# Moving the value sums of a pair of heads to the opening run of the next iteration, with their evacuation and one lower half

## Chip, core, metric

The kernel runs on one core of a Trainium2 chip. The metric is the device time of one execution in microseconds; the time before is 981.24 us, the median of three runs (979.43 to 981.75).

## The reference

Two independent computations, joined along the last axis. Part A is an attention with 32 heads of width 18 over 2048 rows in four segments of 512. Each segment has a causal softmax inside it, plus a lookup in a memory that is summed over the segments before. Part B is a Fourier mixing: two dense matrix products, one over 576 columns and one over 2048 rows. The core of it:

```python
# A: per segment s and head h (L = 512, Dh = 18)
logits = einsum("bhqd,bhkd->bhqk", qs, ks) * Dh**-0.5 + mask   # mask = -1e9 where key > query
a_dot  = einsum("bhqk,bhkd->bhqd", softmax(logits), vs)
a_mem  = einsum("bhld,bhde->bhle", phi(qs), M) / (einsum("bhld,bhd->bhl", phi(qs), z)[..., None] + 1e-6)
o      = sigmoid(beta) * a_mem + (1 - sigmoid(beta)) * a_dot
M, z   = M + phi(ks)^T vs, z + sum(phi(ks))
outA   = concat(o) @ wo
# B
a, b = x @ dft_hid_re.T, x @ dft_hid_im.T
outB = dft_seq_re @ a - dft_seq_im @ b
out  = concatenate([outA, outB], axis=-1)
```

## The kernel before

The first 217 us project queries, keys and values, sum the memory and look it up. From there to about 918 us two things run interleaved: the dense products of part B (`hidden`, then `sequence`, first for the real and then for the imaginary matrix) and the softmax attention of part A. An output stage ends the kernel.

The order is written out by hand. `attention()` is a generator: iteration p works on several pairs of heads at once, each in another stage, and yields eight times. At each yield the main loop makes a tick (which runs what `later(n, ...)` has queued n ticks before), takes what `PLAN` names for that slot, and then puts dense products on TensorE until their share of the work has caught up with the slot's weight in `SLOTS`. So what stands in the text between two yields is issued together, and dense products fill the space between. Of the eight places only two issue TensorE work of the attention in every iteration: the code before the second yield (here called slot 1, the opening run, which begins with `s_fill`) and the code before the fifth (slot 4).

A pair is one even and one odd head. For both, `scores` makes the scores in the PSUM banks `s0`, `s1`, `t0`, `t1`, and `smallest` (line 982, VectorE) takes the row minima of the negated scores. Two groups of heads share the steps:

- Even heads form transposed exponentials. `t_fill` makes the scores and ScalarE their exponentials in `pf` and `phi`; `t_mask` (GpSimd) masks the diagonal blocks; `t_hi` and `t_lo` write the higher halves `phi` and the lower halves `plo` in 16 bits. `t_lo(n, 0)` is VectorE's subtraction over 512 columns, the first lower half; `t_lo(n, 1)` is VectorE's over 384 columns and reads a PSUM bank; `t_lo(n, 2)` runs on GpSimd.
- Odd heads form exponentials with queries on the partitions (`f_fill`, `f_exp`), split them into `hl` (`f_split_hi`, `f_split_lo`) and turn them by a transposing DMA into `ptt` (`f_turn`, on the sync queue).

`pv(n)` (lines 1102, 1103) makes the value sums of one head, 10 products of 55 and 10 of 37 columns; both heads of a pair share the PSUM bank `pv`, of which there is one (`bufs=1`). `pv_out` (lines 1115 to 1124, five VectorE instructions) divides the sums and adds them to the output tile `og`; after the second pair of a group it queues `turn_out`, which transposes `og` (line 1137, VectorE), copies a tail (GpSimd) and sends both out by DMA. A new `pv` may start only when the last instruction of the previous `pv_out` is done.

VectorE has other work in the same stream. The halves of the second Fourier matrix (line 124, `h_split` through `PLAN`, iterations 21 to 29) and the lower halves of `hidden` (line 94) are two. The subtractions of the dense result from the first product (line 654) and the differences for the output stage (lines 744, 715) are the others.

Of the kernel before, what the change touches and what calls it, by code (L numbers as in the profile page):

```python
# [40 lines left out]
def infini_attention_and_fnet(ctx: ExitStack, tc: tile.TileContext, xT, wqk, w8, wv, wo, beta, xtT, cT, hT, out):  # L41
# [46 lines left out]
    def later(n, fn, *a):  # L88
        due.setdefault(clock[0] + n, []).append((fn, a))
# [374 lines left out]
    def stacks(p_, i):  # L464
        qs_bufs.append(p_.tile([P, 4, L], BF16, name=f"qs{i}"))
        ks_bufs.append(p_.tile([P, 4, L], BF16, name=f"ks{i}"))
        pool.memset(ks_bufs[i].bitcast(F32)[96:], BF16_ONES)
# [19 lines left out]

    def stack_load(G):
        if G < NG:
            s, g8 = divmod(G, 8)  # L490
            rows = slice(g8 * 72, g8 * 72 + 72)
            for n, (buf, src) in enumerate(((ks_bufs, kd), (qs_bufs, qd))):
                later(1 + n, dma, buf[G % 4][:NPAIR], src[s][rows].rearrange("(h d) c t -> (d c) h t", d=DH))

    def value_load(G):
        if G < NG:
            s, g8 = divmod(G, 8)
            VS[G] = sa.tile([P, 4, 220], BF16, name="vst", bufs=2)
            dma(VS[G], vd[s][:, :, g8])
# [65 lines left out]
    def bank(name, shape, dtype, tag):  # L565
        turns[tag] ^= 1
        return ps.tile(shape, dtype, name=name, tag=f"{tag}{turns[tag]}", bufs=1)
# [397 lines left out]
    def scores(n, kind, tag="s"):  # L965
        G, h = divmod(n, 4)
        q, k = qs_bufs[G % 4][:NPAIR, h], ks_bufs[G % 4][:NPAIR, h]
        if kind == 2 and SHARED:
            o = SHARED.pop()
        else:  # L970
            o = bank("s", [P, L], F32, tag)
            if kind == 2:
                SHARED.append(o[:, 256:])
        for i, c in ROWS[kind]:
            w = (i + 1) * P
            pe.matmul(o[:, c:c + w], q[:, i * P:w], k[:, :w], start=True, stop=True)  # L976
        return o
# [7 lines left out]
    def s_fill(n, kind, o=None):  # L985
        G, h = divmod(n, 4)
        smallest(scores(n, kind) if o is None else o, kind, -1.0, NEGM[G % 2][:, 2 * h:2 * h + 4])
# [3 lines left out]
    def f_fill(n, kind, o=None):  # L991
        if o is None:
            o = scores(n, kind, "s" if kind else "t")
        if kind == 1:
            F_[n] = [sa.tile([P, 4], F32, name="nb", bufs=2), sa.tile([P, 1280], F32, name="pf", bufs=3), {}]
        smallest(o, kind, -SCALE, F_[n][0])
        F_[n][2][kind] = o
# [27 lines left out]
    def maxima(G):  # L1025
        m, b = NEGM[G % 2].rearrange("p (h n) -> p h n", h=2), MB[G % 2][:, :24].rearrange("p (h c n) -> p c h n", h=2, c=3)
        r = sa.tile([P, 2, 4], F32, name="negx", bufs=2)
        pool.tensor_copy(b[:, 0], m)
        pool.tensor_tensor(r, m, b[:, 0], OP.subtract)
        pool.tensor_copy(b[:, 1], r)  # L1030
        pool.tensor_tensor(b[:, 2], r, b[:, 1], OP.subtract)

    def maxima_transpose(G, o):
        t = o[:, 384:512]
        pe.matmul(t, MB[G % 2], ident16, start=True, stop=True)
        yield
        w = sa.tile([24, P], BF16, name="mt", bufs=2)
        act.activation(w, t[:24], AF.Copy)
        for h in range(2):
            later(1, dma, qs_bufs[G % 4][NPAIR:NPAIR + 3, 2 * h].rearrange("c (n t) -> c n t", n=4), w[12 * h:12 * h + 12])  # L1040
# [64 lines left out]
    def pv_out(n2):  # L1105
        G, hh = divmod(n2, 2)
        s, g8 = divmod(G, 8)
        o = PV.pop(n2)
        og = OG[G % 2]
        h0 = 4 * g8 + 2 * hh  # L1110
        w = o[:, 440:].rearrange("p (h i c) -> p h i c", h=2, c=1)
        b = o[:, :144].rearrange("p (h i d) -> p h i d", h=2, i=4)
        o = o[:, :440].rearrange("p (h i c) -> p h i c", h=2, i=4)
        a = sa.tile([P, 8, DH], F32, name="pa", bufs=2)
        dve.reciprocal(w, o[:, :, :, 54:])
        dve.tensor_tensor(w, w, g1[:, h0:h0 + 2, None, None].to_broadcast([P, 2, 4, 1]), OP.mult)
        dve.tensor_reduce(a, o[:, :, :, :54].rearrange("p h i (c d) -> p (h i) d c", c=3), axis=AX, op=OP.add)
        to = og[:, :, 36 * hh:36 * hh + 36].rearrange("p i (h d) -> p h i d", d=DH)
        a = a.rearrange("p (h i) d -> p h i d", h=2)
        if s == 0:  # L1120
            dve.tensor_tensor(to, a, w.to_broadcast([P, 2, 4, DH]), OP.mult)
        else:
            dve.tensor_tensor(b, a, w.to_broadcast([P, 2, 4, DH]), OP.mult)
            dve.tensor_tensor(to, to, b, OP.add)
        if hh == 1:
            later(6, turn_out, G)
# [33 lines left out]
    F_LAG, T_LAG, V_LAG = 2, 3, 4  # L1160
    NP = 2 * NG
    SLOTS = (1060.0, 890.0, 1060.0, 660.0, 890.0, 1060.0, 650.0, 1210.0)

    def attention():
        for p in range(NP + V_LAG):
            def even(lag, fn, *a):
                if 0 <= p - lag < NP:
                    fn(2 * (p - lag), *a)

            def odd(lag, fn, *a):  # L1170
                if 0 <= p - lag < NP:
                    fn(2 * (p - lag) + 1, *a)

            if p < 2:
                OG.append(sa.tile([P, 4, 72], F32, name=f"og{p}"))
            if p == 0:
                stack_load(1)
                later(20, value_load, 0)
            if p % 2 == 0:
                later(39, value_load, p // 2 + 1)  # L1180
                later(30, memory_load, p // 2)
            even(T_LAG + 1, t_lo, 0)
            odd(F_LAG + 1, f_split_hi)
            yield SLOTS[0]
            G = p // 2 - 1 if p % 2 == 0 and 0 < p <= NP else None
            even(0, s_fill, 0)
            even(T_LAG, t_fill, 0)
            even(T_LAG, t_fill, 1, G)
            even(0, s_fill, 1)
            if G is not None and p < T_LAG:  # L1190
                list(maxima_transpose(G, bank("trm", [P, L], F32, "t")))
            odd(F_LAG + 1, f_split_lo, pool, 512, 1280)
            yield SLOTS[1]
            even(T_LAG, t_lo, 1)
            odd(F_LAG + 1, f_split_lo, dve, 0, 512)
            yield SLOTS[2]
            if p < 2:
                stacks(sq, p + 2)
            even(T_LAG, t_mask)
            yield SLOTS[3]  # L1200
            SHARED.clear()
            both = {}
            odd(F_LAG, f_fill, 1)
            even(0, lambda n: both.update(s=scores(n, 2)))
            odd(F_LAG, lambda n: both.update(f=scores(n, 2)))
            even(0, lambda n: s_fill(n, 2, both["s"]))
            odd(F_LAG, lambda n: f_fill(n, 2, both["f"]))
            even(V_LAG, pv)
            odd(V_LAG, pv)
            even(T_LAG, t_fill, 2)  # L1210
            odd(F_LAG, f_fill, 0)
            yield SLOTS[4]
            if p % 2 and p < NP:
                maxima(p // 2)
            odd(F_LAG + 1, f_turn)
            if p % 2:
                if p == 1:
                    later(6, stack_load, 2)
                else:
                    stack_load((p + 3) // 2)  # L1220
                if 2 < p < 18:
                    later(2, copy_parts, 2, 7 + p // 2)
            elif 4 <= p < 36:
                later(2, copy_parts, 3, (p - 4) // 2)
            even(T_LAG, t_hi)
            yield SLOTS[5]
            odd(F_LAG, f_exp, 1, 2, 0)
            even(T_LAG, t_lo, 2)
            yield SLOTS[6]
            if V_LAG <= p < NP + V_LAG - 1:  # L1230
                pv_out(p - V_LAG)
            yield SLOTS[7]

    d = dense()
# [6 lines left out]
    for n, w in enumerate(attention()):  # L1241
        tick()
        ta += w
        for fn, a in PLAN.pop(n, ()):
            fn(*a)
        while td / total_d < ta / total_a:
            t = next(d, BREAK)
            if t is BREAK:
                break
            td += t  # L1250
# [56 lines left out]
```

## Time and profile before

| what | value |
| --- | --- |
| median of three runs | 981.24 us |
| the profiled execution, own time | 982.62 us |
| its span, first to last instruction | 980.9 us |
| TensorE busy | 973.3 us (99%) |
| VectorE busy | 749.8 us (76%) |
| ScalarE busy | 680.8 us (69%) |
| GpSimd busy | 663.1 us (68%) |
| granted TensorE clock | 1.0 |
| DMA queue 1, share of 16 engines | 84.8% |

Busy is the union of the recorded instructions. TensorE's ends are modelled, so 99% says that it is rarely without an instruction, not that it runs at its peak. The 1.72 us between the execution's time and its span lie before the first and after the last instruction.

### The profile page before, as it was taken

To read this page: it belongs to the slowest core of one execution; us is meant where nothing else is said; L and a number is where in the kernel's file an instruction comes from. 1 tells how busy PE (TensorE), PEld (TensorE's weight loads), DVE (VectorE), ACT (ScalarE), POOL (GpSimd) and SP (SyncE) were. 2 spreads that over 40 slices of the span, in tenths; PEclk is the share of its full clock that TensorE was granted. 3 is DMA by queue.
4 is the path that set the end of the run, shared out by engine and by line. 5 is a ranking of instruction groups with operands and counts; after the bars stand their busy time and mean duration, and the time that the engine had idled before them with its cause. 6 is when DMAs were issued, how large, how long until landed. Compare 5 with 4: busy or idle time off the path is not lost.

```text
span 980.9 us, 25226 instructions
## 1 busy us (share of the span) xinstructions
PE 973.3 (99%) x9246; PEld 921.8 (94%) x9246; DVE 749.8 (76%) x2113; ACT 680.8 (69%) x1559; POOL 663.1 (68%) x746
## 2 busy tenths in 40 slices
PE   9999999999999999999999999999999999999998
PEld 7989989899999999999999999999999999999998
DVE  6657668585677877788888778878888789887785
ACT  7757576564886776867778677776777767768442
POOL 2658577686767666776776776667677877776561
PEclk9999999999999999999999999999999999999999
DMA  7537557775888899899999998899999999998663
GB/s 247 190 117 242 204 167 246 237 250 171 192 189 227 209 240 240 214 234 233 242 240 236 233 213 188 187 208 224 230 228 249 225 236 255 243 208 175 178 195 119
DMA packets 304349, 209.95 MB, mean 214 GB/s; under 512 B 204992, under 2 KB 259136, under 8 KB 304192
## 3 DMA queue, kind: packets, MB, share of 16 engines
q1 hardware_dynamic: 304000, 208.20, 84.8%
q8 instruction: 72, 1.18, 0.5%
q14 instruction: 53, 0.43, 0.1%
q10 hardware_dynamic: 224, 0.14, 0.0%
HBM read 122.37 MB, written 58.98 MB: 185 GB/s over the span
## 4 chain that ended last, share of the span: by engine, by line
PE 90%; DMA 5%; ACT 2%; POOL 2%; DVE 1%; issue 1%; SPq 0%; POOLq 0%; ACTq 0%
PE d L584 35%; PE s L976 6%; PE v L84 6%; PE qk L84 6%; PE qk L251 5%; PE pv L1102 4%; DMA ptt<-hl 4%; PE d L629 3%; PE d L630 3%; PE d L631 3%; PE t L869 2%; PE pv L1103 2%; PE d L869 2%; PE s L869 2%; PE m L364 1%; PE t L1053 1%
## 5 line engine op out<-in xcount | busy, mean ns | idle before, releaser
L982 DVE CUSTOM_DVE_ANT_0 s<-s,causal 128x128 f32<-128x128 f32 (+3 forms) x512 | 247.9, 507 | 76.2 <-PE s L976 67.3
L457 POOL TENSOR_TENSOR clo<-craw,chi 128x512 fp32r<-128x512 f32 x159 | 219.3, 1380 | 115.2 <-ACT chi L452 97.4
L584 PE MATMUL d<-wide,chi 128*128 128x288 f32 x1408 | 256.9, 300 | 0.0
L584 PEld LDWEIGHTS d<-wide,chi 128*128 128x128 f32 x1408 | 211.4, 188 | 0.7
L584 PE MATMUL d<-wide,clo 128*128 128x288 f32 x704 | 168.3, 306 | 0.0
L1066 ACT ACTIVATE phi<-t 128x384 f16<-128x384 f32 x128 | 62.4, 488 | 139.0 <-PE t L1063 139.0
L1018 POOL TENSOR_TENSOR hl<-pf,hl 128x768 f16<-128x768 f32 x64 | 108.5, 1695 | 34.0 <-ACT hl L1014 22.6
L584 PE MATMUL d<-ab,chi 128*128 128x288 f32 x640 | 121.0, 299 | 0.0
L584 PEld LDWEIGHTS d<-wide,clo 128*128 128x128 f32 x704 | 118.5, 188 | 0.9
L1005 ACT ACTIVATE pf<-s,nb 128x128 f32<-128x128 f32 (+3 forms) x256 | 114.1, 529 | 2.1
L976 PE MATMUL s<-ks,qs 108*128 108x128 bf16 (+3 forms) x512 | 112.8, 302 | 0.5 <-DVE negm L982 0.5
L452 ACT ACTIVATE chi<-craw 128x512 fp32r<-128x512 f32 x160 | 101.5, 635 | 3.1 <-DMA craw<-xtT 1.8
L584 PEld LDWEIGHTS d<-ab,chi 128*128 128x128 f32 x640 | 97.9, 188 | 0.3
L1014 ACT ACTIVATE hl<-pf 128x768 f16<-128x768 f32 (+1 forms) x128 | 88.2, 751 | 0.0
L584 PE MATMUL d<-ab,clo 128*128 128x288 f32 x320 | 81.3, 303 | 0.0
L1085 POOL TENSOR_TENSOR plo<-pf,phi 128x384 f16<-128x384 f32 x64 | 63.4, 990 | 25.5 <-ACT pf L1070 23.6
L629 PE MATMUL d<-wide,chi 128*128 128x288 f32 x256 | 78.5, 307 | 0.0
L630 PE MATMUL d<-wide,chi 128*128 128x288 f32 x256 | 75.7, 296 | 0.0
L631 PE MATMUL d<-wide,clo 128*128 128x288 f32 x256 | 75.6, 295 | 0.0
L1070 ACT ACTIVATE pf<-t 128x512 f32<-128x512 f32 (+1 forms) x128 | 70.0, 547 | 7.8 <-PE t L1053 7.1
L1085 DVE TENSOR_TENSOR plo<-pf,phi 128x512 f16<-128x512 f32 x64 | 60.9, 951 | 0.3 <-ACT phi L1079 0.3
L976 PEld LDWEIGHTS <-qs 108*128 108x128 bf16 x512 | 41.9, 98 | 18.4 <-issue 0.7
(286 smaller groups left out, 2558.1 us busy)
## 6 DMA issues: line engine op xcount, KB each, us to landing
craw<-cT SPq DMA_DIRECT2D x128, 256.0 KB
ks<-kd SPq DMA_DIRECT2D x32, 432.0 KB
qs<-qd SPq DMA_DIRECT2D x32, 432.0 KB
craw<-xtT SPq DMA_DIRECT2D x32, 320.0 KB
vd<-vs SPq DMA_DIRECT2D x16, 440.0 KB
vst<-vd SPq DMA_DIRECT2D x32, 220.0 KB
qd<-p SPq DMA_DIRECT2D x16, 384.0 KB
kd<-p SPq DMA_DIRECT2D x16, 384.0 KB
```

What stands on the lines that cost most here:

```text
L84: pe.matmul(o, a, b, start=n == 0, stop=n == len(terms) - 1)
L452: act.activation(hi, raw[:, :4], AF.Copy)
L457: engine.tensor_tensor(lo, raw[:, :4], hi.bitcast(F32), OP.subtract)
L584: pe.matmul(o[h], a, b[:, h * 288:h * 288 + 288], start=start, stop=stop)
L629: pe.matmul(o, xh[:, k], wl[k][:, cs], start=k == 0, stop=False)
L630: pe.matmul(o, xh[:, k], wh[k][:, cs], start=False, stop=False)
L631: pe.matmul(o, xl[:, k], wh[k][:, cs], start=False, stop=False)
L976: pe.matmul(o[:, c:c + w], q[:, i * P:w], k[:, :w], start=True, stop=True)
L982: dve.tensor_tensor_reduce(o[:, c:c + w], o[:, c:c + w], CAUSAL[0][:, L - w:], scale=scale, scalar=-LOWEST, op0=OP.add, op1=OP.min, accum_ ...
L1005: act.activation(f[:, FIRST_COL[i]:FIRST_COL[i] + w], o[kind][:, c:c + w], AF.Exp, bias=nb[:, i:i + 1], scale=-1.0)
L1018: engine.tensor_tensor(hl[:, 1, a:b], f[:, a:b], hl[:, 0, a:b], OP.subtract)
L1085: (pool if kind == 2 else dve).tensor_tensor(lo[:, a:b], f, hi[:, a:b], OP.subtract)
```

## The change

Three steps move and nothing is added or left out.

- `pv` of both heads of a pair leaves slot 4 of iteration p, where it stood between the scores and the last transposed scores. It stands now at the head of slot 1 of iteration p + 1, ahead of `s_fill`. The last pair has its `pv` in iteration 67 itself, before the seventh yield.
- `pv_out` moves with it, from before the last yield of iteration p to before the seventh yield of iteration p + 1 (one slot earlier in the iteration, one iteration later). `turn_out`, which it queues six ticks ahead, moves along.
- `t_lo(n, 0)`, the first lower half, moves from the first slot of an iteration (before the first yield) to the fourth (after `t_mask`).

```diff
@@ attention(), iteration p
-            even(T_LAG + 1, t_lo, 0)
             odd(F_LAG + 1, f_split_hi)
             yield SLOTS[0]
             G = p // 2 - 1 if p % 2 == 0 and 0 < p <= NP else None
+            even(V_LAG + 1, pv)
+            odd(V_LAG + 1, pv)
             even(0, s_fill, 0)
...
             even(T_LAG, t_mask)
+            even(T_LAG + 1, t_lo, 0)
+            if p == NP + V_LAG - 1:
+                pv_out(NP - 2)
             yield SLOTS[3]
...
             odd(F_LAG, lambda n: f_fill(n, 2, both["f"]))
-            even(V_LAG, pv)
-            odd(V_LAG, pv)
             even(T_LAG, t_fill, 2)
             odd(F_LAG, f_fill, 0)
             yield SLOTS[4]
...
             even(T_LAG, t_lo, 2)
+            if V_LAG < p < NP + V_LAG - 1:
+                pv_out(p - V_LAG - 1)
+            if p == NP + V_LAG - 1:
+                even(V_LAG, pv)
+                odd(V_LAG, pv)
             yield SLOTS[6]
-            if V_LAG <= p < NP + V_LAG - 1:
-                pv_out(p - V_LAG)
             yield SLOTS[7]
```

On TensorE, a steady iteration in the first Fourier half, before: the four score products of slot 4, then `pv`, then the last transposed scores (line 1062) and dense products (line 584).

```order
L976 LDWEIGHTS qs_3054
L976 MATMUL s<-ks_3055,qs_3054 128x256
L1102 LDWEIGHTS phi
L1102 MATMUL pv<-vst,phi 128x55
...
L1103 MATMUL pv<-vst,ptt 128x37
L1062 LDWEIGHTS ks_2920
L1062 MATMUL t<-qs_2919,ks_2920 128x128
```

The same place in the changed kernel: dense products stand ahead of `pv`, and the 512-column scores of `s_fill` and the scores of `t_fill` (line 1053) behind it.

```order
L584 MATMUL d<-ab,clo 128x288 x2
L1102 LDWEIGHTS phi
L1102 MATMUL pv<-vst,phi 128x55
...
L1103 MATMUL pv<-vst,ptt 128x37
L976 LDWEIGHTS qs_2430
L976 MATMUL s<-ks_2431,qs_2430 128x512
L1053 LDWEIGHTS ks_3055
L1053 MATMUL t<-qs_3054,ks_3055 128x128
```

The run of 80 instructions has moved as one block from the middle of slot 4 to the head of slot 1.

On VectorE, iteration 25 of the generator before, from the last minima of slot 4 on: a lower half of the second Fourier matrix (`wide`), the five instructions of `pv_out`, the first lower half (`plo<-pf`), then the first minima of the next slot 1 (`negm`).

```order
L982 ISA s,nb<-s,causal 128x512
L982 ISA nb 128x1
L124 TENSOR_TENSOR wide<-raw,wide 128x576
L1115 RECIPROCAL pv<-pv 128x8
L1116 TENSOR_TENSOR pv<-pv,g_118 128x8
L1117 TENSOR_REDUCE pa<-pv 128x144
L1123 TENSOR_TENSOR pv<-pa,pv 128x144
L1124 TENSOR_TENSOR og_2866<-og_2866,pv 128x2x4x18
L1085 TENSOR_TENSOR plo<-pf,phi 128x512
L982 ISA s,negm_2424<-s,causal 128x512
```

The same iteration in the changed kernel, first the piece ahead of the minima of slot 4: the second lower half (`plo<-t`), a lower half of `hl`, then the first lower half and the transposes of `og`, both new here.

```order
L1085 TENSOR_TENSOR plo<-t,phi 128x384
L1018 TENSOR_TENSOR hl<-pf,hl 128x512
L1085 TENSOR_TENSOR plo<-pf,phi 128x512
L1137 STREAM_TRANSPOSE ogt<-og_2996 128x128 x2
L982 ISA s,nb<-s,causal 128x128
```

And the piece behind those minima, with `pv_out` still behind the lower half of the Fourier matrix.

```order
L982 ISA s,nb<-s,causal 128x512
L982 ISA nb 128x1
L124 TENSOR_TENSOR wide<-raw,wide 128x576
L1115 RECIPROCAL pv<-pv 128x8
L1116 TENSOR_TENSOR pv<-pv,g_118 128x8
L1117 TENSOR_REDUCE pa<-pv 128x144
L1123 TENSOR_TENSOR pv<-pa,pv 128x144
L1124 TENSOR_TENSOR og_2866<-og_2866,pv 128x2x4x18
L982 ISA s,negm_2424<-s,causal 128x512
```

The first lower half has gone from behind `pv_out` to ahead of slot 4's minima, and in every second iteration the two transposes of `og` stand there too; before, these stood behind the minima of the other iterations.

## Prediction

> **What bounds the kernel now.** I read the page first, then TensorE's waits, then the rows of the transposed tile, then the rows of single iterations engine by engine.
>
> ```profile
> span 980.9 us, 25226 instructions
> PE 973.3 (99%) x9246; PEld 921.8 (94%) x9246; DVE 749.8 (76%) x2113; ACT 680.8 (69%) x1559; POOL 663.1 (68%) x746
> ```
>
> TensorE has something in flight for 99% of the span, so a change that moves its work without adding any can gain only what it waits. The waits of TensorE, as engine, line, what it waited for, total us, times, longest:
>
> ```profile
> PE pv L1102 <- DMA ptt<-hl: 1.6, 3, 0.8
> PE warm L240 <- DVE ones L68: 1.1, 1, 1.1
> PE s L976 <- DVE negm L982: 0.5, 1, 0.5
> PE qk L251 <- ACT wide L130: 0.2, 1, 0.2
> PE t L1053 <- DMA qs<-mt: 0.2, 1, 0.2
> ```
>
> Two of the five are within the change's reach: `pv` waiting for the turned exponentials, and scores waiting for minima that were late. No row has `pv` waiting for VectorE: the single `pv` bank has always been evacuated in time. The rows of the turned tile give the first wait by the weight loads, which are not modelled:
>
> ```profile
> L1023 SPq DMA_TRANSPOSE ptt<-hl x64: 2976/4021/6726, 253.3 to 909.8; - x64
>   PEld L1102: 2.1, 4
> ```
>
> **What is removed.** The turned tile gets more time. It is waited for in slot 4 now and in the next slot 1 afterwards. The two openings stand here, from one steady iteration of TensorE (start, length, then the instruction):
>
> ```profile
> 480.24 0.61 PE L976 MATMUL s<-ks,qs 108*128 108x128 bf16 x4
> 480.69 0.19 PE L1102 MATMUL pv<-vst,phi 128*128 128x55 bf16 x1
> ...
> 481.72 0.22 PE L1062 MATMUL t<-qs,ks 111*128 111x128 bf16 x1
> ...
> 486.89 0.39 PE L976 MATMUL s<-ks,qs 108*128 108x512 bf16 x1
> ...
> 490.71 0.61 PE L976 MATMUL s<-ks,qs 108*128 108x128 bf16 x4
> ...
> 492.35 0.38 PE L976 MATMUL s<-ks,qs 108*128 108x512 bf16 x1
> ```
>
> Slot 4 opens at 480.24, the next slot 1 at 486.89, the next slot 4 at 490.71. `pv` takes 481.72 - 480.69 = 1.03 us. In the new place it starts 486.89 - 1.03 - 480.69 = 5.2 us later than now. The longest wait above is 0.8 us, so all of them go: a gain of 1.6 us by TensorE's idle time, 2.1 by the weight loads. I take 2.1. The wait for `negm` (0.5) came where evacuation and first lower half lay ahead of slot 1's minima; both leave that place, so it goes too. Gain: 2.1 + 0.5 = 2.6 us, the ends 1.6 and 3.1 (the five waits end behind modelled tails of 0.19 us, which could hide up to 0.5 more).
>
> **What is moved on VectorE.** The rows of that iteration on VectorE, and of the start of the next:
>
> ```profile
> 480.67 0.30 DVE L982 CUSTOM_DVE_ANT_0 s<-s,causal 128x128 f32<-128x128 f32 x1
> ...
> 483.10 0.76 DVE L124 TENSOR_TENSOR wide<-raw,wide 128x576 fp32r<-128x576 f32 x1
> 483.77 0.21 DVE L1115 RECIPROCAL pv<-pv 128x8 f32<-128x8 f32 x1
> ...
> 485.21 0.30 DVE L1124 TENSOR_TENSOR og<-og,pv 128x144 f32<-128x144 f32 x1
> 485.44 0.68 DVE L1085 TENSOR_TENSOR plo<-pf,phi 128x512 f16<-128x512 f32 x1
> ...
> 489.07 0.56 DVE L1085 TENSOR_TENSOR plo<-t,phi 128x384 f16<-128x384 f32 x1
> ...
> 491.14 0.30 DVE L982 CUSTOM_DVE_ANT_0 s<-s,causal 128x128 f32<-128x128 f32 x1 [0.92 <-PE s L976]
> ...
> 493.57 0.50 DVE L1137 STREAM_TRANSPOSE ogt<-og 128x128 f32<-128x128 f32 x2
> 494.00 0.18 DVE L1115 RECIPROCAL pv<-pv 128x8 f32<-128x8 f32 x1
> ```
>
> The minima of slot 4 begin 0.43 us after its opening (480.67) and hold VectorE for 483.10 - 480.67 = 2.43. The evacuation takes 485.21 + 0.30 - 483.77 = 1.74. In an iteration with nothing between them it would end 0.43 + 2.43 + 1.74 = 4.60 us after the opening. The next `pv` must start 6.65 - 1.03 = 5.62 after it (6.65 is the distance of the openings now, and 1.03 goes out of slot 4). That leaves 1.0 us where the old order, with the next `pv` at 10.47 + 0.45 = 10.9 us, left over 5. Into this 1.0 us come:
>
> - the first lower half, 0.68 us, now ahead of slot 4's minima; its mean over the kernel is 0.95, from the row below;
> - in every second iteration the two transposes, 494.00 - 493.57 = 0.43, ahead of the minima as well;
> - what stays between minima and evacuation, here 483.77 - 483.10 = 0.67.
>
> ```profile
> L1085 DVE TENSOR_TENSOR plo<-pf,phi 128x512 f16<-128x512 f32 x64 | 60.9, 951 | 0.3 <-ACT phi L1079 0.3
> ```
>
> Against them stands VectorE's idle time ahead of slot 4's minima: 0.92 us at 491.14, none at 480.67. Between the two I take 0.4 for a steady iteration. So: without transposes 1.0 - (0.68 - 0.4) = 0.7 us to spare, no wait. With them 1.0 - (1.11 - 0.4) = 0.3, hardly a wait; I put 0.3 us on all of these together. In the iteration shown, with no idle time and the Fourier half, 1.0 - 1.11 - 0.67 = -0.8: `pv` waits 0.8 us. Everything on TensorE stands behind it, so this is time.
>
> Five iterations with transposes (four of line 124, one of line 127) have such a Fourier half ahead of the evacuation. The shortest distance of openings makes one worse:
>
> ```profile
> 439.85 0.61 PE L976 MATMUL s<-ks,qs 108*128 108x128 bf16 x4
> 445.18 0.39 PE L976 MATMUL s<-ks,qs 108*128 108x512 bf16 x1
> ```
>
> 5.33 us, 1.3 less than the usual, against an idle time of 0.8 there: 1.1 us. The five come to 1.1 + 0 + 0.8 + 0.9 + 0.7 = 3.5 us, worked for each from its own two openings as above.
>
> The last Fourier product (the final 23 iterations) is the larger part. One of its iterations, TensorE's openings and then VectorE:
>
> ```profile
> 817.98 0.61 PE L976 MATMUL s<-ks,qs 108*128 108x128 bf16 x4
> 824.77 0.39 PE L976 MATMUL s<-ks,qs 108*128 108x512 bf16 x1
> ```
>
> ```profile
> 819.19 0.28 DVE L982 CUSTOM_DVE_ANT_0 s<-s,causal 128x128 f32<-128x128 f32 x1
> ...
> 821.61 0.46 DVE L744 TENSOR_TENSOR raw<-raw 128x288 f32<-128x288 f32 x1
> 822.58 0.46 DVE L654 TENSOR_TENSOR y<-y,d 128x288 f32<-128x288 f32 x1 [0.52 <-PE d L584]
> ```
>
> The minima begin 1.21 us after the opening, already late. Add 1.11, then 2.43 for the minima, 0.46 for the difference, 0.46 for the subtraction that the new order still has ahead, and 1.74: 7.4 us. `pv` wants its bank at 6.79 - 1.03 = 5.76, so it waits 1.6. Ten of the 23 iterations have a wait when worked this way, most of them with transposes and a subtraction or difference ahead, from 0.1 to 1.6 us and 0.7 in the mean: 7 us.
>
> Sum of new waits: 3.5 + 7 + 0.3 = 10.8, of which I take 10, since lateness in the last stretch comes partly from the lower half that no longer stands ahead of slot 1. The ends: 4 us if most of that lateness goes, 17 us if the lower half costs its mean of 0.95 in its new place too (0.27 more in nearly every iteration, which turns the 0.3 to spare into nothing).
>
> **Weighed against the skill.** The row first: none of TensorE's waits above is `pv` on VectorE, with one bank and 64 pairs. The Trainium skill, "Perfetto Trace Analysis", section "Matmuls", says that independent groups of products should rotate through different banks, so that an evacuation lies beside the next group's products. By that rule alone every pair would pay its evacuation, an estimate of 63 x 1.74 = 110 us. The trace of before does not bear that out, since dense products in other banks fill the time; it would hold only for the part of an evacuation that reaches past the dense run.
>
> **What else moves, at nothing.** The last scores of slot 4 lose the cover of `pv`: they need the bank that the second lower half reads. That ends at 489.63, and the scores at 492.35 come 1.03 earlier, so 1.7 us are left. The transposing DMA now needs a `pv` of the same iteration to be done; the SyncE row says when it is issued, and the load of the next `og`, behind the transposes and GpSimd's copy, comes later still:
>
> ```profile
> 490.57 6.15 SPq L1023 DMA_TRANSPOSE ptt<-hl  x1
> 484.46 0.57 SPq L1158 DMA_DIRECT2D og<-amd  x1
> 483.60 1.78 ACT L1005 ACTIVATE pf<-s,nb 128x128 f32<-128x128 f32 x4
> ```
>
> `pv` ends at slot 1's opening, about 486.9, and the DMA is issued at 490.57: 3.7 us of cover. The load stands 484.46 - 480.24 = 4.2 us behind the opening, the transposes now end within 2. If either cover went, the sync queue would stand still, and the loads of dense operands behind it.
>
> **The sum.** -2.6 + 10 = +7.4 us on the profiled execution's 982.62 us (span 980.9), so 990.0. That execution lies 1.4 us above the median, so the forecast in the median's terms is 988.6.
>
> **Rivals.**
>
> 1. Not slower: the covers hold. VectorE is 24% idle; if minima and evacuations run earlier in the new order by the 0.8 us or so that a bad iteration lacks, only the gain is left: 981.24 - 2.6 = 978.6, or 981.24 - 3.1 = 978.1 with the waits' hidden tails. For it: steady iterations have 0.3 to 0.7 us to spare by the sum above. Against it: 480.67 has no idle time at all. It decides at 1.0 us of added work per iteration.
> 2. Slower through another door: the minima come late, so ScalarE's exponentials (483.60 + 1.78 = 485.38) free the score banks late. The opening at 486.89 gives 1.5 us, and the delay is 0.7 to 1.1, so it decides only in iterations as late as 819.19. Ten of these at 0.5 us more would add 5: 993.6.
> 3. No effect that shows: `pv` waits about as long for its bank as it waited for the DMA. With the low end of new waits, 4, less 2.6, that is 982.6. For it: the lateness of the last stretch may go with the lower half. Against it: the 3.5 us of the Fourier halves don't hang on that.
>
> **How the numbers follow.** Forecast 0.68, rivals 0.14, 0.08 and 0.10. A measurement of this kernel tells about 0.3% (2.9 us) from no change, which is 978.3 to 984.2. Slower by more: the forecast but for its lowest tail, and rival 2, 0.74. Within: rival 3, most of rival 1 and that tail, 0.20. Faster by more: rival 1 with its largest gain, 0.06. The range runs from 980 (between rivals 1 and 3) to 995 (new waits of 17 less 2.6, or rival 2).
>
> **What would show it.** In the changed profile TensorE's waits should have no row of `pv` on the DMA of `ptt`, and a new row of `pv` line 1102 on `og` line 1124, some 15 times, about 10 us together, the longest near 1.6, none in the first 16 pairs. VectorE's idle time ahead of slot 4's minima should shrink and that ahead of slot 1's grow. Wrong it would be if that row is missing or under 4 us (the evacuation's place), if scores wait for line 1005 (rival 2), or if TensorE waits no longer and the time has still risen (something that I don't see).

## Result and profile after

The changed kernel takes 1016.55 us (median of 5 runs, 1014.56 to 1019.01), the kernel before 980.91 us beside it. The ratio is 1.0345, 95% interval 1.0318 to 1.0371: slower by 3.5%, where 0.75% was predicted.

The head of the page, and the four largest of TensorE's waits (engine, line, what it waited for, total us, times, longest):

```profile
span 1015.1 us, 25275 instructions
PE 980.3 (97%) x9246; PEld 926.4 (91%) x9246; DVE 771.3 (76%) x2113; ACT 689.6 (68%) x1559; POOL 674.9 (66%) x746
```

```profile
PE pv L1102 <- DVE og L1124: 19.5, 23, 2.0
PE pv L1102 <- DVE og L1121: 4.9, 8, 1.1
PE d L584 <- DVE y L654: 4.0, 3, 1.7
PE warm L240 <- DVE ones L68: 1.1, 1, 1.1
```

The rows of `pv` on `ptt` and of scores on `negm` are gone. In their place `pv` waits for its bank in 31 places, 24.4 us by these rows. By the starts of the products (what the step from the last dense product to the first `pv` takes beyond its usual length) it is 30.6 us. A third row is new as well: dense products wait for VectorE's subtraction, 4.0 us. The new waits less the 2.1 us of the rows that are gone make 32.5 of the 34.2 us by which the two spans differ (1015.1 - 980.9).

One VectorE instruction of every iteration has changed its length, the first lower half. Line 1085 grouped by form (duration in ns, shortest, median, longest), first of the kernel before, then of the changed one, then the changed page's row with the mean:

```profile
L1085 DVE TENSOR_TENSOR plo<-pf,phi x64: 681/746/2056, 259.1 to 911.9; 128x512 f16<-128x512 f32 x64
```

```profile
L1085 DVE TENSOR_TENSOR plo<-pf,phi x64: 676/1412/1791, 264.1 to 948.2; 128x512 f16<-128x512 f32 x64
```

```profile
L1085 DVE TENSOR_TENSOR plo<-pf,phi 128x512 f16<-128x512 f32 x64 | 82.3, 1286 | 0.0
```

The same subtraction of 512 columns takes 1.29 us in the mean in its new place, against 0.95 before, and it comes in steps: 0.68, 1.1, 1.4, 1.77. An early iteration, without transposes and without any Fourier work between minima and evacuation, shows what that does. Below are rows of TensorE, then of VectorE, then of GpSimd, each with start, length and instruction:

```profile
309.27 0.61 PE L976 MATMUL s<-ks,qs 108*128 108x128 bf16 x4
...
315.61 0.19 PE L1102 MATMUL pv<-vst,phi 128*128 128x55 bf16 x1 [0.57 <-DVE og L1121]
...
316.63 0.38 PE L976 MATMUL s<-ks,qs 108*128 108x512 bf16 x1
```

```profile
309.43 0.68 DVE L1018 TENSOR_TENSOR hl<-pf,hl 128x512 f16<-128x512 f32 x1
310.03 1.78 DVE L1085 TENSOR_TENSOR plo<-pf,phi 128x512 f16<-128x512 f32 x1
311.73 0.29 DVE L982 CUSTOM_DVE_ANT_0 s<-s,causal 128x128 f32<-128x128 f32 x1
...
314.15 0.21 DVE L1115 RECIPROCAL pv<-pv 128x8 f32<-128x8 f32 x1
...
315.25 0.30 DVE L1121 TENSOR_TENSOR og<-pa,pv 128x144 f32<-128x144 f32 x1
```

```profile
309.49 1.77 POOL L457 TENSOR_TENSOR clo<-craw,chi 128x512 fp32r<-128x512 f32 x1 [0.25 <-ACT chi L452]
```

Slot 4 opens at 309.27. The lower half holds VectorE until 311.81, 2.5 us past the opening, so the minima start at 311.73 instead of some 0.5 us behind the opening, the evacuation ends at 315.55, and `pv` waits. The prediction gave an iteration of this kind 0.7 us to spare.

Why 1.78? GpSimd's subtraction for the dense operands (line 457, two tiles of SBUF read, as in the lower half) ends at 309.49 + 1.77 = 311.26, and the lower half ends 0.55 us later. Beside nothing on GpSimd it takes 0.68: 4 of the 64 in this trace, 19 of 64 before. With the mask (line 1074) and line 457 beside it, it takes 1.76 in the mean of 15. Where GpSimd's instruction began after it, the trace has 0.68 again. All 64 places fit one pattern. In 50 a GpSimd instruction had begun before the lower half and was still running; there the lower half ends 0.54 to 0.56 us after that instruction, whichever it was. In the other 14 it takes 0.68. So the rows look like turn-taking: whichever began first reads, the other stands still.

The Trainium skill, "SBUF — State Buffer", section "Who interferes with whom", states this as a rule: a VectorE instruction with two SBUF inputs and a GpSimd instruction that reads SBUF take turns, the later one is blocked until the first is done; with one SBUF input, outside VectorE's two-port modes, there is no conflict. The rows above agree on two inputs; one input is tried in a run below.

### The profile page after: what moved, and what is told of

Same layout as the page of the kernel before. It is cut to its first block, busy times and chain, and to the rows that moved or that the text cites. A ratio compares the mean times of both kernels' runs of the same rounds, so it can differ in the third digit from the quotient of the medians.

```text
span 1015.1 us, 25275 instructions
## 1 busy us (share of the span) xinstructions
PE 980.3 (97%) x9246; PEld 926.4 (91%) x9246; DVE 771.3 (76%) x2113; ACT 689.6 (68%) x1559; POOL 674.9 (66%) x746
## 4 chain that ended last, share of the span: by engine, by line
PE 58%; DVE 29%; ACT 10%; issue 3%; POOL 1%; DVEq 0%; POOLq 0%; ACTq 0%
DVE s L982 11%; PE d L584 11%; DVE plo L1085 8%; PE v L84 6%; PE qk L84 6%; PE qk L251 5%; PE pv L1102 3%; PE d L629 3%; PE d L630 3%; PE d L631 3%; DVE hl L1018 3%; PE s L976 3%; ACT pf L1005 3%; PE t L869 2%; ACT hl L1014 2%
## 5 line engine op out<-in xcount | busy, mean ns | idle before, releaser
L457 POOL TENSOR_TENSOR clo<-craw,chi 128x512 fp32r<-128x512 f32 x159 | 224.1, 1409 | 124.0 <-ACT chi L452 88.3
L1018 POOL TENSOR_TENSOR hl<-pf,hl 128x768 f16<-128x768 f32 x64 | 106.0, 1657 | 45.4 <-ACT hl L1014 29.9
L1085 DVE TENSOR_TENSOR plo<-pf,phi 128x512 f16<-128x512 f32 x64 | 82.3, 1286 | 0.0
L1001 ACT ACTIVATE nb<-nb 128x4 f32<-128x4 f32 x64 | 13.1, 205 | 82.1 <-DVE nb L982 81.6
```

The costliest lines, as they stand in the source:

```text
L457: engine.tensor_tensor(lo, raw[:, :4], hi.bitcast(F32), OP.subtract)
L1018: engine.tensor_tensor(hl[:, 1, a:b], f[:, a:b], hl[:, 0, a:b], OP.subtract)
L1085: (pool if kind == 2 else dve).tensor_tensor(lo[:, a:b], f, hi[:, a:b], OP.subtract)
```

## Experiments

Three theories stood against each other. Theory A: the one `pv` bank is evacuated too late, because the first lower half stands ahead of slot 4's minima and is long there. Theory B: the short window between one pair's sums and the next minima is enough by itself, whatever the lower half does. Theory C: late minima make the exponentials late, these free the score banks late, and the wait for the `pv` bank is only a symptom.

**The lower half put back.**

```diff
+            even(T_LAG + 1, t_lo, 0)
             odd(F_LAG + 1, f_split_hi)
...
             even(T_LAG, t_mask)
-            even(T_LAG + 1, t_lo, 0)
```

> The changed kernel with the first lower half put back at the head of slot 1; the value sums and their evacuation stay where the change put them. Theory A (the single pv bank is evacuated too late because the first lower half, 1.29 us in its new place, stands ahead of slot 4's minima): nearly all of the 35 us goes, 979 to 986 us, TensorE's row of pv on og under 5 us in under 10 places. Theory B (the short 5.6 us between one pair's sums and the next's minima is enough by itself, whatever the lower half does): 1000 us or more, the row of pv on og still above 15 us. Theory C (late minima make exponentials and scores late, the bank is a symptom): 979 to 986 too, since the minima are no longer late.

Measured 986.67 us, ratio 1.0037 (1.0016 to 1.0057). Its one row of `pv`, by TensorE's waits:

```profile
PE pv L1102 <- DVE og L1124: 4.1, 6, 1.7
```

B is out: 30 of the 35 us went with this one instruction. The time lies 0.7 us above the range that A and C gave. What is left, six waits of the bank and a total 4.5 us above the kernel before beside it, I put down to the window; no run tests that alone.

**The lower half alone, in two designs.**

```diff
-            even(T_LAG + 1, t_lo, 0)
...
             even(T_LAG, t_mask)
+            even(T_LAG + 1, t_lo, 0)
...
-            even(V_LAG, pv)
-            odd(V_LAG, pv)
             even(T_LAG, t_fill, 2)
             odd(F_LAG, f_fill, 0)
+            even(V_LAG, pv)
+            odd(V_LAG, pv)
```

> The kernel before with one part of the change alone: the first lower half in the fourth slot, behind the mask. The value sums stand at the end of slot 4's run instead of its middle, so that they need not wait for the lower half, and the evacuation stays at the end of the iteration, with 5 us to spare. Theory A: no wait for the bank, 980 to 986 us, although the first lower half takes about 1.3 us here too. Theory B: the same, 980 to 986. Theory C: the minima are as late as in the changed kernel (1.6 us behind slot 4's opening), so most of the loss comes back: 1000 us or more.

The second design puts the two `pv` lines ahead of `yield SLOTS[5]` instead.

> The kernel before with the first lower half in the fourth slot, as the run e2_lo_alone, but with the value sums one slot later still (ahead of the exponentials of slot 6), so that they do not wait for the lower half directly, which ends 1.4 us behind slot 4's opening; evacuation at the end of the iteration. Theory A: neither the bank nor the lower half is waited for, 980 to 986 us. Theory C: the minima are 1 us later than before, 1000 us or more.

Measured 1030.09 us, ratio 1.0491 (1.0463 to 1.0520), and 1005.57 us, ratio 1.0243 (1.0228 to 1.0259). The row of `pv` in each:

```profile
PE pv L1103 <- DVE plo L1085: 35.1, 50, 1.9
```

```profile
PE pv L1103 <- DVE plo L1085: 13.7, 20, 1.5
```

Both numbers are C's, the mechanism isn't: the sums wait for the lower half itself, which is their operand. I had made too little room for it, so these two don't test A. Nor do they speak for C: the minima of the second start 1.75 us behind slot 4's opening in the mean, later than in the changed kernel, and no score waits for the exponentials. In the second the waits explain only part of the loss; TensorE's busy time is 10.8 us higher as well (984.1 against 973.3), where the sums stand in another run.

**Half of it moved.**

```diff
-        a, b = ((0, 512), (512, 896), (896, 1280))[kind]
+        a, b = ((0, 256), (512, 896), (896, 1280), (256, 512))[kind]
...
+            even(T_LAG + 1, t_lo, 3)
             odd(F_LAG + 1, f_split_hi)
```

> The changed kernel with only half of the first lower half (256 of 512 columns) in the fourth slot, the other 256 columns at the head of slot 1. Theory A: the work ahead of slot 4's minima falls by some 0.6 of 1.29 us; about two thirds of the 39 waits are shorter than that by the rows (longest 2.0), so 988 to 1000 us, and pv on og 5 to 14 us. Theory B: 1005 to 1015. Theory C: about half of the loss, 993 to 1003.

Measured 997.77 us, ratio 1.0164 (1.0138 to 1.0190).

```profile
PE pv L1102 <- DVE og L1124: 11.0, 19, 1.4
PE pv L1102 <- DVE og L1121: 2.0, 4, 0.9
```

Half the columns bring about half of the loss and half of the bank's waits (13.0 of 24.4 us). A's range held, and C's too, so this run doesn't part them.

**The evacuation moved instead.** Ahead of slot 4's minima:

```diff
             even(T_LAG + 1, t_lo, 0)
-            if p == NP + V_LAG - 1:
-                pv_out(NP - 2)
+            if V_LAG < p < NP + V_LAG:
+                pv_out(p - V_LAG - 1)
...
-            if V_LAG < p < NP + V_LAG - 1:
-                pv_out(p - V_LAG - 1)
```

> The changed kernel with the evacuation moved ahead of slot 4's minima (right behind the first lower half in the fourth slot), everything else as changed. The minima are now later by another 1.7 us, and the bank is free some 2 us earlier. Theory A: the row of pv on og is gone and with it most of the loss: 980 to 990 us. Theory B: 980 to 990 too. Theory C: the minima are the cause, so it is slower than the changed kernel: 1020 us or more.

And directly behind them (`pv_out(p - V_LAG - 1)` behind `odd(F_LAG, f_fill, 0)`):

> The changed kernel with the evacuation directly behind slot 4's minima, ahead of the turned split and the Fourier halves that stood between them; the minima are as late as in the changed kernel (1.6 us behind slot 4's opening, with the first lower half ahead). The mean iteration of the changed kernel has 5.70 - 2.61 - 1.74 = 1.35 us between minima and evacuation, so the bank is free up to 1.35 us earlier. Theory A (the bank): of the 31 waits of 0.8 us in the mean most go, 980 to 992 us, pv on og under 6 us. Theory C (late minima hurt by exponentials and scores): as the changed kernel, 1010 to 1020.

Measured 1095.80 us, ratio 1.1154 (1.1127 to 1.1180), and 1021.76 us, ratio 1.0405 (1.0388 to 1.0423). The three largest of TensorE's waits in the first, then in the second:

```profile
PE s L976 <- ACT pf L1005: 33.9, 34, 1.8
PE d L584 <- DVE y L654: 16.9, 6, 3.7
PE t L1035 <- ACT pf L1005: 8.6, 20, 2.2
```

```profile
PE d L584 <- DVE y L654: 11.5, 5, 3.2
PE pv L1102 <- DVE og L1124: 9.8, 17, 1.1
PE pv L1102 <- DVE og L1121: 4.1, 8, 0.8
```

A's numbers fell in both. In the first the bank is free, as A said, but the minima start 3.7 us behind the opening in the mean, and what C describes happens: scores wait for the exponentials of line 1005. In the changed kernel (1.65 us behind) no such row exists, so C's mechanism is real but is not what slows the changed kernel. In the second the bank's waits fell by 10.5 us and those of the dense products rose by 7.5 and more: the evacuation now stands ahead of VectorE's subtraction `y`. All waits together are the same there, 30.1 us against 30.0 in the changed kernel.

In both runs the granted clock was lower too: 0.982 and 0.991 in the profiled executions, against 0.998 in the changed kernel, with TensorE busy for 1009.7 and 985.5 us against 980.3. So part of the first run's loss, and possibly all of the 5 us by which the second is above the changed kernel, is not waiting; why the clock was lower stays open.

My 1.35 us between minima and evacuation were wrong as well: they counted four of slot 4's five minima. By the five, other work stands there for 0.3 us in the mean of 59 iterations, for none in most and for 1.2 at most.

**The transposes behind the minima** (`later(7, turn_out, G)` for `later(6, ...)`).

> The changed kernel with the two transposes of every second iteration behind slot 4's minima instead of ahead of them, still ahead of the evacuation. The minima come 0.43 us earlier in these iterations and the evacuation ends at the same time. Theory A: unchanged, 1012 to 1019 us. Theory C: 5 us or more faster, 1005 to 1011.

Measured 1020.14 us, ratio 1.0392 (1.0372 to 1.0411).

```profile
PE pv L1102 <- DVE og L1124: 22.8, 25, 2.1
PE pv L1102 <- DVE og L1121: 5.2, 7, 1.3
```

The minima start 1.44 us behind the opening in the mean, 0.2 earlier than in the changed kernel, and the kernel is not faster but a little slower (A's range is missed by 1 us, C's by 9). Earlier minima are worth nothing while the evacuation ends no earlier. That speaks against C as the cause here, for the bank.

**Everything that made the bank late taken back.** The lower half at the head of slot 1, the evacuation directly behind the minima, `later(7, turn_out, G)`.

> The value sums in slot 1 as in the changed kernel, with all that made their bank late taken back: the first lower half at the head of slot 1, the evacuation directly behind slot 4's minima, the transposes behind it. The bank should be free some 4.2 us behind slot 4's opening, against 5.6 when it is wanted. Theory A: no wait for the bank and none for the turned exponentials, so the 2.6 us of gain that the prediction worked out are left, 977 to 981 us. Theory B (the window is too short by itself): 984 or more. Theory C: 977 to 981 as well, since the minima are as early as before.

Measured 987.25 us, ratio 1.0053 (1.0034 to 1.0072). A and C missed; B's number is met, but not by its wait:

```profile
PE d L584 <- DVE y L654: 5.2, 4, 1.7
PE t L1053 <- DMA qs<-mt: 2.3, 1, 2.3
PE warm L240 <- DVE ones L68: 1.1, 1, 1.1
PE pv L1102 <- DVE og L1124: 0.2, 1, 0.2
```

The bank is hardly waited for any more, and `ptt` not at all. In their place dense products wait 5.2 us for the subtraction that the evacuation overtook. The 2.3 us for one load may belong to this execution alone, which at 990.74 us is the slowest of the four. In the last stretch VectorE is late for one of the two, whichever stands second; that is read from these rows and from those of the run with the evacuation directly behind the minima.

**Why the lower half is long.** First its place: the lower half in the second slot, ahead of `t_lo(n, 1)`.

```diff
+            even(T_LAG + 1, t_lo, 0)
             even(T_LAG, t_lo, 1)
...
             even(T_LAG, t_mask)
-            even(T_LAG + 1, t_lo, 0)
```

> The changed kernel with the first lower half in the second slot, ahead of the second one (which waits 24.1 us in 25 places for ScalarE there), and not in the fourth; value sums and evacuation as changed. If the loss comes from what stands between the last scores of slot 3 and slot 4's minima, these start 0.5 us behind the opening again, and most of the loss goes: 980 to 988 us, pv on og under 6 us. If any late place of the lower half delays the evacuation, because VectorE has no idle time to absorb it: 995 us or more.

Measured 997.47 us, ratio 1.0160 (1.0140 to 1.0180), in the range of the second guess, that any late place delays the evacuation. `pv` waits 8.3 us for its bank in 15 places.

```profile
L1085 DVE TENSOR_TENSOR plo<-pf,phi 128x512 f16<-128x512 f32 x64 | 64.3, 1005 | 0.0
```

The lower half takes 1.0 us in the mean there, and VectorE's wait for ScalarE absorbed only part of it. Then the mask beside it:

```diff
-        act.activation(to, o[:, :w], AF.Exp, bias=LIFT, scale=SCALE)
+        act.activation(to, o[:, :w], AF.Exp, bias=LIFT, scale=SCALE if kind else 0.05 * SCALE)
...
-            even(T_LAG, t_mask)
             even(T_LAG + 1, t_lo, 0)
```

This kernel leaves out the mask and scales the exponents of the diagonal blocks down.

> The changed kernel without GpSimd's mask of the diagonal blocks, which runs beside the first lower half in the fourth slot; left out are the mask and, so that the numbers stay finite, 95% of the exponent of the diagonal blocks; every other instruction is the same. If the lower half takes 1.76 us because GpSimd works beside it (0.68 where it doesn't), its mean falls from 1.29 to 1.05 us or less and the time to 1000 to 1010 us. If it is slow for another reason in this place (what it waits for, where its operands lie), mean and time stay: 1.25 us or more, 1012 to 1019 us.

Measured 1015.77 us, ratio 1.0347 (1.0330 to 1.0363).

```profile
L1085 DVE TENSOR_TENSOR plo<-pf,phi 128x512 f16<-128x512 f32 x64 | 83.8, 1309 | 0.0
```

By its numbers this spoke for the place. Its rows didn't: line 457 had moved up into the mask's time, and where it began ahead of the lower half, the lower half took about the time to the end of line 457 plus 0.55; where GpSimd did nothing beside, 0.68 in 8 of 8. Taking one of GpSimd's instructions away doesn't empty its queue. So the next run changes the instruction itself.

**One tile read instead of two,** in the new place and, as a control, in the old one:

```diff
+        if kind == 0:
+            dve.tensor_reduce(lo[:, a:b], f.rearrange("p (c o) -> p c o", o=1), axis=AX, op=OP.max)
+            return
         (pool if kind == 2 else dve).tensor_tensor(lo[:, a:b], f, hi[:, a:b], OP.subtract)
```

> The changed kernel with the first lower half in its new place as an instruction that reads one tile of SBUF instead of two (a copy of 512 columns by a reduction over one element each; the subtraction of the upper half is left out). If the lower half is long because it and GpSimd's subtraction take turns at reading, it takes one length in all 64 places, about 0.6 to 0.7 us, the minima of slot 4 start 1.0 us behind the opening instead of 1.6, and the time is what the prediction worked out with 0.68 us: 986 to 994 us. If it is long because of its place or its wait, the mean stays above 1.2 us and the time at 1012 to 1019.

> The kernel before with the same one-tile instruction in the lower half's old place, at the head of slot 1 (the subtraction of the upper half is left out). Control for the run before it: its mean falls from 0.95 to 0.6 to 0.7 us, and since TensorE does not wait for it in that place, the time stays within 2 us of before, 980 to 983 us.

Measured 991.38 us, ratio 1.0086 (1.0061 to 1.0110), and for the control 981.26 us, ratio 0.9989 (0.9974 to 1.0005). In the new place (the added lines move `pv` to 1105 and `og` to 1127), the group of the instruction, TensorE's wait, and the same iteration as above on VectorE and GpSimd:

```profile
L1086 DVE TENSOR_REDUCE plo<-pf x64: 669/678/681, 264.0 to 923.0; 128x512 f16<-128x512 f32 x64
```

```profile
PE pv L1105 <- DVE og L1127: 6.4, 10, 1.2
```

```profile
308.22 0.68 DVE L1018 TENSOR_TENSOR hl<-pf,hl 128x512 f16<-128x512 f32 x1
308.82 0.68 DVE L1086 TENSOR_REDUCE plo<-pf 128x512 f16<-128x512 f32 x1
309.42 0.29 DVE L982 CUSTOM_DVE_ANT_0 s<-s,causal 128x128 f32<-128x128 f32 x1
```

```profile
308.28 1.75 POOL L457 TENSOR_TENSOR clo<-craw,chi 128x512 fp32r<-128x512 f32 x1 [0.26 <-ACT chi L452]
```

GpSimd's line 457 runs beside it here too (1.75 us), and the instruction takes 0.67 to 0.68 us in all 64 places: the place alone does not make it long. The edit takes away the second tile and the subtraction together; that it is the second read and not the subtraction follows from the 50 places above, where the length hangs on GpSimd's end, and from the 0.68 that the subtraction takes without it. The minima start 0.9 us behind the opening in the mean, against 1.65. 25.2 us of the loss go with it (1016.55 - 991.38). In the old place the same edit is worth nothing that can be measured.

**The gain without the cost.** In the kernel before, only the odd head's sums later (ahead of `yield SLOTS[5]`):

> The kernel before with only the odd head's value sums (which read the turned tile) one slot later, ahead of the exponentials of slot 6; the even head's sums, the evacuation and the lower half stay. The waits for the turned tile are at most 0.8 us, the sums stand some 2 us later, and the evacuation at the end of the iteration keeps over 2 of its 5 us to spare. Gain of the change without its cost: 977 to 980 us, no row of pv on ptt. If the waits for the turned tile were covered elsewhere anyway: within 1.5 us of before.

Then both heads' sums behind `odd(F_LAG, f_fill, 0)`, at the end of slot 4's run:

> The kernel before with both heads' value sums at the end of slot 4's run instead of in its middle, 1 us or more later; the lower half, the evacuation and all else as before. The waits for the turned tile are 0.8 us at most, so they go, the bank keeps over 3 us to spare, and the run is not split in two: 978 to 980.5 us, no row of pv on ptt. If scores and transposed products in slot 4 have to wait for their banks once the sums no longer stand between them: 981 us or more, with a new row of s or t.

Measured 986.89 us, ratio 1.0053 (1.0038 to 1.0067), and 985.55 us, ratio 1.0028 (1.0013 to 1.0043). The busy times of the engines in the first, then all of TensorE's waits in the second:

```profile
PE 978.7 (99%) x9246; PEld 922.9 (94%) x9246; DVE 750.2 (76%) x2113; ACT 686.6 (70%) x1559; POOL 662.3 (67%) x746
```

```profile
PE warm L240 <- DVE ones L68: 1.1, 1, 1.1
PE s L976 <- DVE negm L982: 0.4, 1, 0.4
```

The waits for the turned tile went and the time rose, against what was expected; the new row of `s` or `t`, which the second text named for a slower case, is not there either. By the starts of TensorE's products, the first dense product that resumes behind another run takes 0.29 us to the next start in the kernel before, not the usual 0.13. That kernel has 136 such places, with 21.6 us above the usual; with the odd head split off there are 197, with 26.4. These 4.8 us are three quarters of what has to be explained (4.0 by which the products take longer from first to last, and 2.4 of waits gone). In the second, the sums follow a product of 512 columns by 0.22 us where they followed one of 256 by 0.11 (6.8 us in 62), and the transposed products, which followed a short `pv` by 0.03, follow that one by 0.11 (5.1 us); the dense products get 6.5 back. With the 2.5 us of waits gone that makes 2.9, by which the products take longer. This is read from the traces and not tested by a run; why the first dense product takes longer stays open. No version here that does all the work beats the kernel before.

## Why the prediction was wrong

The direction and the mechanism were right, the size wasn't: 988.6 predicted (980 to 995), 1016.55 measured.

- **The gain** held as far as waits go. No wait on `ptt` or `negm` is left in the trace after. The prediction took 2.1 us over 1.6 because the weight loads "are not modelled"; the traces don't show that (the 1280 of line 1102 all last 0.09 to 0.10 us in the kernel before), but only 0.5 us hang on it.
- **The step that failed** is the first term of "What is moved on VectorE": "the first lower half, 0.68 us, now ahead of slot 4's minima; its mean over the kernel is 0.95". It measured 1.29 in the mean. I took the price from the old place, where GpSimd did nothing beside it in 19 of 64, and the old place's mean as the upper end. In the new place that holds for 4 of 64, and in 50 GpSimd was already at work. What the runs showed instead: the length is the time to the end of GpSimd's instruction plus 0.55 us, up to 1.79. With 0.68 in that place (the one-tile run) the kernel takes 991.4, inside the range, with 10 waits of 6.4 us by the rows and 17 of 9.5 us by the starts. The prediction said 15 and 10. Of the 28 us by which it missed, 25 are this term.
- **No wait in the first 16 pairs**, and the steady iteration with 0.3 to 0.7 us to spare: wrong with 1.78 us in it (8 waits of the row on line 1121), right with 0.68, where that row is missing.
- **The upper end**, 17 us of waits, came from 0.27 us more in nearly every iteration, the excess of a mean. The excess comes in steps of up to 1.1 us, and with 1.0 to spare it is the steps that count. A slip besides: the worst of the five Fourier iterations comes to 1.3 us by the terms that stand beside it (0.8 + 1.3 - 0.8), not 1.1; this moves the sum by 0.2.
- **The row that was not foreseen**, dense products on `y` (4.0 us): the prediction saw that subtraction only as something ahead of the evacuation. The run with only the evacuation moved behind the minima shows that the two compete for the same late VectorE: 10.5 us less for the bank, 7.5 more for the subtraction.
- **Rivals.** That exponentials free the score banks late is not in the trace after, with minima 1.65 us late in the mean; the run with 3.7 us has it. That the covers hold (rival 1) fell with the lower half. That no effect would show (rival 3) fell likewise.

## What to carry to other kernels

An instruction's price belongs to its place: before moving one that reads two SBUF tiles on VectorE, look at what GpSimd reads there. Price it by the slowest step of its durations, not by their median or mean. Where a stage has 1 us to spare, a move is decided by such steps. Taking away a wait that TensorE shows is no gain by itself; here two orders without it were slower.

## What the runs showed of the hardware

The turn-taking reaches further than one pair of instructions. In the iteration shown, GpSimd's line 457 was recorded from 309.49, while VectorE's `hl` was reading (from 309.43, 0.68 us). Its record of 1.77 us is 0.5 longer than the usual 1.29 (the median of 159), and it went ahead of the lower half that VectorE issued next. In this trace `hl` stands directly ahead of the lower half in 50 iterations; in 43 of them a GpSimd instruction began during `hl` and ran on, and in 41 of these the lower half ended only 0.54 to 0.56 us after it. Two such VectorE instructions in a row thus let GpSimd in between them, and both engines' records hold the time they stood still.
